# A plan with engine clocks decides the order of issue of routing lists and experts

## Chip, cores and metric

One core of a Trainium2 chip. The metric is the device time of one execution in microseconds (us). TensorE (PE), VectorE (DVE), ScalarE (ACT) and GpSimd (POOL) each run their own instructions in the order in which the program issues them, and wait for one another by semaphores; SyncE (SP) issues most plain transfers.

## What is computed

- Stage A: a two-dimensional Fourier transform of x (8 x 3072 x 256), of which the real part is kept, and the first expert layer, `((x @ w1) * (x @ w2)) @ w3 @ w_out`, for 24576 tokens.
- Stage B, which the change touches: routing and eight experts.

```
logits = x @ w_gate                       # 24576 tokens x 8 experts
for (tok, e) in descending order of logit:
    if tok is free and expert e has fewer than 3072 tokens: assign tok to e
for e in range(8):
    h = max(x[mask_e] @ w1[e], 0);  out[mask_e] = h @ w2[e]
```

The kernel finds the assignment in eight rounds ("lists"): in each one it finds the expert that fills up first and which tokens it takes, then takes that expert and those tokens out.

## The kernel before

**A list** (`route`, line 1122, a generator) has these parts. The set-up (lines 1130 to 1165, VectorE) makes each token's best logit, its expert and a 16-bit key in two halves, and two transposing transfers on SP's queue. Two searches (`search`, line 1094) of eight rounds each look for a threshold; a round is two counts on VectorE (line 1087, 1536 and 864 columns) beside two on ScalarE (line 1084), two small matmuls that add the counts up (lines 1102 and 1103, called "sums" here), and three small VectorE operations that choose the next threshold (lines 1109, 1111, 1114), on which the next counts wait. After the searches, lines 1193 to 1217 choose the expert and mark its tokens, lines 1226 to 1258 number them (with matmuls 1233, 1239, 1242), and lines 1267 to 1283 turn marks into a list of row numbers: three parts, each some 20 VectorE operations, one on ScalarE and 64 small matmuls ("matches", in bursts of 16). Line 1288 writes the finished list `idx`. The eighth list takes whatever is left and has no searches.

**The experts** (loop at line 1590): 8 experts x 6 groups of 512 tokens x 8 steps. A step is `first` (line 1447): six matmuls of 512 columns into `hp`, whose ReLU ScalarE writes as a high half (line 1467) and VectorE as a low half (line 1471); then `second` (line 1478) of the step two before: twelve matmuls of 256 columns. In the second step of each group GpSimd makes the low half instead (line 1462). At steps 4 and 6 `turned` (line 1430) transposes the next group's rows, which ScalarE and VectorE split into halves (lines 1437 and 1441). `chunk` (line 1395) splits a piece of the next expert's weights (ScalarE, then GpSimd), `gather` and `store` fetch and write rows by GpSimd's indirect transfers.

**The head**: the first list has no experts to run beside; TensorE fills it with matmuls that stage A put off (`putoff`, line 1339, matmuls at line 1376), and their operands come back from memory.

**The order** of all instructions is written out by the program itself (`manual_schedule`, line 1556). The list generator yields an estimated VectorE cost after each piece, -2 ahead of matmuls that need VectorE's or ScalarE's result, and -1 after a burst of matches. `lists()` (line 1527), called four times a step, goes on with the list while the estimated clock of VectorE is at most QUEUE ahead of TensorE's, returns after each -1, and at a -2 while the clocks of VectorE or ScalarE are ahead of TensorE's. The two counts of a round are charged 0.95 + 0.45 and 0.6 us on VectorE's clock (lines 1087 to 1088). The halves of `hp` and of the transposed rows are issued a fixed number of calls of `due()` later. At the start of an expert's last group whatever is missing of the next list is issued at once (line 1594).

Of the kernel before, what the change touches and what calls it, by code (L numbers as in the profile page):

```python
# [9 lines left out]
F32 = mybir.dt.float32  # L10
# [12 lines left out]
NT = N // 128  # L23
# [995 lines left out]
def stage_b(ctx, tc, I, out, k):  # L1019
# [16 lines left out]
    CHAIN = 0.45  # L1036
# [27 lines left out]
    clock = {"pe": 0.0, "v": 0.0, "a": 0.0, "d": 0.0}  # L1064

    def use(engine, cost, after=0.0):
        clock[engine] = max(clock[engine], after) + cost
        return clock[engine]


# [3 lines left out]
    def count(T, nx):  # L1074

        acc = cnt[0]
        cnt.reverse()
        ja = rt.tile([128, E * NT], BF, name="ja", bufs=1)  # L1080
        for i, n in enumerate((E * NT, SHARE)):
            a = slice(0, E * NT) if i == 0 else slice(SHARE, E * NT)
            with nc.allow_low_precision(reason="counts of at most 1536 are exact"):
                act.activation(ja[:, a], T[:, a], AF.Sign, bias=nx[:, 2 + i:3 + i], accum_out=acc[:, 2 + 3 * i:3 + 3 * i])  # L1084
            use("a", 1.65 if i == 0 else 0.95)
            jk = junk[i]
            vec.tensor_scalar(jk[:, :n], T[:, :n], nx[:, i:i + 1], None, op0=ALU.is_ge, op1=ALU.add, accum_out=acc[:, i:i + 1])  # L1087
            yield 0.95 + CHAIN if i == 0 else 0.6
        return acc
# [4 lines left out]
    def search(T, thr, name, res, extra):  # L1094

        cur, nx = zero, cc[:, 0]
        for i in range(8):
            acc = yield from count(T, nx)
            yield -2
            then = extra[i]() if i in extra else None  # L1100
            ps = rps(4)
            nc.tensor.matmul(ps, blk, acc[:, 0:4], start=True, stop=False)
            nc.tensor.matmul(ps, half, acc[:, 4:8], start=False, stop=True)
            if then:
                then()
            ps = ps[:, 0:3]
            if i < 7:
                bn = small([5], "bn")
                vec.scalar_tensor_tensor(bn, sg5, cur, cc[:, i + 1], op0=ALU.mult, op1=ALU.add)
            kk, j3 = small([1], "kk"), small([3], "j3")  # L1110
            vec.scalar_tensor_tensor(j3, ps, 1.0, thr, op0=ALU.mult, op1=ALU.is_ge, accum_out=kk)
            if i < 7:
                nx = small([5], "nx")
                vec.scalar_tensor_tensor(nx, sv[:, i], kk, bn, op0=ALU.mult, op1=ALU.add)  # L1114
                cur = nx[:, 4:5]
            else:
                new = small([1], name)
                vec.scalar_tensor_tensor(new, kk, 1.0, cur, op0=ALU.mult, op1=ALU.add)
                cur = new
        res.append(cur)  # L1120

    def route(ph, done):
# [3 lines left out]
        if ph < E - 1:  # L1126

            v = rt.tile([128, NT], F32, name="v", bufs=1)
            v4 = rt.tile([128, 8, NT], BF, name="C8", bufs=1).rearrange("p a j -> p (a j)").bitcast(F32).rearrange("p (a j) -> p a j", a=4)
            vec.tensor_tensor(v4, Lw[:, 0:4], Lw[:, 4:8], op=ALU.max)  # L1130
            vec.tensor_tensor(v4[:, 0:2], v4[:, 0:2], v4[:, 2:4], op=ALU.max)
            vec.tensor_tensor(v, v4[:, 0], v4[:, 1], op=ALU.max)
            yield 1.7
            oh = rt.tile([128, E, NT], BF, name="X8", bufs=1)
            vec.tensor_tensor(oh, Lw, v[:, None, :].to_broadcast(whole(E)), op=ALU.is_equal)
            yield 1.7
            vec.tensor_tensor(oh, oh, rank, op=ALU.mult)
            yield 0.9
            m4 = rt.tile([128, 8, NT], BF, name="C8", bufs=1)[:, :4]
            vec.tensor_tensor(m4, oh[:, 0:4], oh[:, 4:8], op=ALU.max)  # L1140
            vec.tensor_tensor(m4[:, 0:2], m4[:, 0:2], m4[:, 2:4], op=ALU.max)
            code = rt.tile([128, NT], BF, name="code", bufs=1)
            vec.tensor_tensor(code, m4[:, 0], m4[:, 1], op=ALU.max)
            yield 1.0
            vec.tensor_tensor(oh, oh, code[:, None, :].to_broadcast(whole(E)), op=ALU.is_equal)
            yield 0.9

            vi = v.bitcast(I32)
            ky = rt.tile([128, NT], I32, name="ky", bufs=1)
            vec.tensor_scalar(ky, vi, 31, -2147483648, op0=ALU.arith_shift_right, op1=ALU.bitwise_or)  # L1150
            vec.tensor_tensor(ky, ky, vi, op=ALU.bitwise_xor)
            hl = rt.tile([128, 2, NT], U16, name="hlv", bufs=1)
            vec.tensor_tensor(hl, ky.bitcast(U16).rearrange("p (j h) -> p h j", h=2), alive[:, None, :].to_broadcast(whole(2)), op=ALU.mult)
            yield 0.9
# [6 lines left out]
            for i, T in ((1, hT), (0, lT)):  # L1161
# [3 lines left out]
                nc.sync.dma_start(T.rearrange("p (k t) -> p k t", k=12), pl, transpose=True)  # L1165
                yield 0.9
                use("d", 0.0, clock["v"] + 3.4)
            yield -2
# [6 lines left out]
            vec.tensor_scalar(hb, hc, -1.0, -0.5, op0=ALU.mult, op1=ALU.add)  # L1175
            with nc.allow_low_precision(reason="counts of at most 1536 are exact"):
                act.activation(junk[0], hT, AF.Sign, bias=hb, accum_out=acc[:, 2:3])
            vec.scalar_tensor_tensor(lT, hT, hc, lT, op0=ALU.is_equal, op1=ALU.mult)
            yield 1.7
            thr2 = small([3], "thr2")  # L1180

            def rest(acc=acc):
                ps = rps(4)
                nc.tensor.matmul(ps, blk, acc[:, 0:4], start=True, stop=True)
                base = small([1], "base")
                vec.tensor_scalar(base, ps[:, 2:3], 0.5, float(8 * E * NT), op0=ALU.mult, op1=ALU.add)
                vec.scalar_tensor_tensor(thr2, neg3, base, thr1, op0=ALU.mult, op1=ALU.add)

            yield from search(lT, thr2, "lc", res, {0: rest})
# [3 lines left out]
            vec.tensor_scalar(d8[:, 0], id8, hc, None, op0=ALU.mult)  # L1193
            vec.scalar_tensor_tensor(d8[:, 1], id8, lc, id8, op0=ALU.mult, op1=ALU.add)
            yield 0.4
            yield -2
            ps = rps(2 * E)
            nc.tensor.matmul(ps, onesf, d8.rearrange("p a e -> p (a e)"), start=True, stop=True)
            t8 = rt.tile([128, 2, E], F32, name="t8")
            vec.tensor_copy(t8.rearrange("p a e -> p (a e)"), ps)  # L1200
            mh, ml, l8 = small([1], "mh"), small([1], "ml"), small([E], "l8")
            vec.tensor_reduce(mh, t8[:, 0], axis=AX.X, op=ALU.max)
            vec.scalar_tensor_tensor(l8, t8[:, 0], mh, t8[:, 1], op0=ALU.is_equal, op1=ALU.mult)
            vec.tensor_reduce(ml, l8, axis=AX.X, op=ALU.max)
            vec.scalar_tensor_tensor(l8, l8, ml, rank9[:, :E], op0=ALU.is_equal, op1=ALU.mult)
            vec.tensor_reduce(ec, l8, axis=AX.X, op=ALU.max)
            vec.tensor_scalar(ml, ml, 1.0, None, op0=ALU.subtract)
# [24 lines left out]
        for c in range(3):  # L1232
            nc.tensor.matmul(tot[:, c * 128:(c + 1) * 128], m2[:, c * 128:(c + 1) * 128], ones, start=True, stop=True)
# [417 lines left out]
```

## Time and profile before

| what | us |
|---|---|
| time, median of 3 runs | 2791.53 (2791.46 to 2792.09) |
| time of the profiled execution | 2802.85 |
| its span, first to last instruction | 2801.1 |
| stage A ends, the head begins | 1395 |
| first expert's first matmul | 1527 |
| last matmul | 2790 |

Positions are us from the start of the span. The profiled execution is 11.3 us longer than the median of the runs; sums are made against the profiled one and then set back by those 11.3 us. A matmul's end in the trace is modelled, and matmuls overlap: what one costs is the distance between starts.

### The profile page before, as it was taken

To read this page: it belongs to the slowest core of one execution; us is meant where nothing else is said; L and a number is where in the kernel's file an instruction comes from. 1 tells how busy PE (TensorE), PEld (TensorE's weight loads), DVE (VectorE), ACT (ScalarE), POOL (GpSimd) and SP (SyncE) were. 2 spreads that over 40 slices of the span, in tenths; PEclk is the share of its full clock that TensorE was granted. 3 is DMA by queue.
4 is the path that set the end of the run, shared out by engine and by line. 5 is a ranking of instruction groups with operands and counts; after the bars stand their busy time and mean duration, and the time that the engine had idled before them with its cause. 6 is when DMAs were issued, how large, how long until landed. Compare 5 with 4: busy or idle time off the path is not lost.

```text
span 2801.1 us, 51732 instructions
## 1 busy us (share of the span) xinstructions
PE 2666.7 (95%) x19903; PEld 2451.8 (88%) x19903; DVE 2130.4 (76%) x3711; ACT 1317.3 (47%) x2383; POOL 1524.3 (54%) x1529
## 2 busy tenths in 40 slices
PE   4999999999999999999996999989999999999998
PEld 2899999999999999987796888878888888889997
DVE  8788787978878797898877888788787878862222
ACT  2344444444444444444453747555573746543332
POOL 7295775939577593964304345353635436363532
PEclk8999999999999999999997999999999999999999
DMA  6410110111111011145394112211212122121211
GB/s 232 134 54 32 39 47 25 49 37 50 36 39 47 24 47 39 45 159 200 133 330 164 43 61 57 69 50 46 75 45 70 50 67 56 41 69 43 76 46 35
DMA packets 104705, 207.33 MB, mean 74 GB/s; under 512 B 35178, under 2 KB 60442, under 8 KB 99338
## 3 DMA queue, kind: packets, MB, share of 16 engines
q1 hardware_dynamic: 81000, 131.03, 13.7%
q0 software_dynamic: 22224, 72.58, 8.1%
q8 instruction: 157, 2.57, 0.4%
q14 instruction: 90, 0.74, 0.1%
q10 hardware_dynamic: 1234, 0.41, 0.1%
HBM read 118.16 MB, written 80.28 MB: 71 GB/s over the span
## 4 chain that ended last, share of the span: by engine, by line
PE 76%; DVE 15%; issue 3%; ACT 3%; POOL 2%; DMA 1%; another core or an unknown queue 0%; DVEq 0%; POOLq 0%; ACTq 0%; SPq 0%
PE yp L1488 14%; PE l L221 7%; PE l L223 7%; PE l L222 7%; PE hp L221 5%; PE acc L805 5%; PE hp L222 5%; PE hp L223 5%; PE acc L801 4%; PE acc L802 4%; DVE oR L1087 3%; PE l L837 3%; PE hp L1376 1%; ACT ja L1084 1%; DVE qs L860 1%
## 5 line engine op out<-in xcount | busy, mean ns | idle before, releaser
L855 POOL TENSOR_TENSOR al<-qs,ah 128x512 fp32r<-128x512 f32 x376 | 513.2, 1365 | 404.7 <-ACT ah L854 316.4
L1488 PE MATMUL yp<-FA,W 128*128 128x256 f32 x3040 | 621.3, 286 | 15.4 <-DVE W L1471 7.5
L1488 PEld LDWEIGHTS yp<-FA,W 128*128 128x128 f32 x3040 | 496.8, 190 | 37.2 <-DVE W L1471 10.4
L860 DVE TENSOR_TENSOR qs<-pm 128x512 f32<-128x512 f32 x384 | 427.1, 1112 | 41.2 <-DVE pm L844 1.8
L1471 DVE SCALAR_TENSOR_TENSOR W<-hp,W 128x512 fp32r<-128x512 f32 x336 | 230.4, 687 | 233.6 <-ACT W L1467 217.8
L854 ACT ACTIVATE ah<-qs 128x512 fp32r<-128x512 f32 x376 | 237.2, 631 | 354.4 <-DVE qs L860 309.9
L1488 PE MATMUL yp<-FB,W 128*128 128x256 f32 x1520 | 387.4, 282 | 0.0
L843 DVE TENSOR_TENSOR pm<-l,qs 128x512 f32<-128x512 f32 x384 | 264.7, 689 | 150.8 <-PE l L223 117.4
L841 ACT ACTIVATE qs<-l 128x512 f32<-128x512 f32 x384 | 227.3, 592 | 239.2 <-PE l L223 223.9
L221 PE MATMUL hp<-tabA,tabB 128*128 128x512 f32 x768 | 318.1, 414 | 0.9 <-ACT tabA L1437 0.9
L1467 ACT ACTIVATE W<-hp 128x512 fp32r<-128x512 f32 x336 | 199.5, 594 | 253.2 <-PE hp L223 227.3
L1498 POOL DMA_INDIRECT out_dram<-yo,oi x188 | 193.3, 1028 | 223.4 <-DMA out_dram<-yo,oi 210.4
L222 PE MATMUL hp<-tabA,tabB 128*128 128x512 f32 x768 | 303.8, 396 | 8.3 <-DVE tabA L1441 8.3
L1084 ACT ACTIVATE ja<-oR,nx 128x1536 bf16<-128x1536 uint16 x196 | 238.1, 1215 | 139.8 <-DVE nx L1114 125.8
L1488 PEld LDWEIGHTS yp<-FB,W 128*128 128x128 f32 x1520 | 287.4, 189 | 14.3
L801 PE MATMUL acc<-W,ah 128*128 128x264 f32 x1120 | 283.7, 284 | 0.0
L1087 DVE TENSOR_SCALAR_CACHE_REDUCE oR<-oR,nx 128x1536 uint16<-128x1536 uint16 x196 | 280.8, 1460 | 3.5
L802 PE MATMUL acc<-W,ah 128*128 128x264 f32 x1120 | 283.4, 284 | 0.0
L844 DVE TENSOR_TENSOR pm<-l,qs 128x512 f32<-128x512 f32 x384 | 261.1, 680 | 0.0
L1412 POOL DMA_INDIRECT xt<-xs_d,idx x192 | 201.4, 1049 | 109.2 <-issue 50.8
L1462 POOL TENSOR_TENSOR W<-xo,W 128x512 fp32r<-128x512 f32 x48 | 62.1, 1293 | 340.2 <-ACT W L1460 315.1
L223 PE MATMUL hp<-tabA,tabB 128*128 128x512 f32 x624 | 246.0, 394 | 0.0
(346 smaller groups left out, 6894.8 us busy)
## 6 DMA issues: line engine op xcount, KB each, us to landing
xs_d<-xo SPq DMA_DIRECT2D x96, 260.0 KB
xt<-in_xg_dram SPq DMA_DIRECT2D x24, 1024.0 KB
away<-ah SPq DMA_DIRECT2D x56, 256.0 KB
away<-al SPq DMA_DIRECT2D x56, 256.0 KB
yo<-away SPq DMA_DIRECT2D x28, 512.0 KB
raw<-in_w3t_dram SPq DMA_DIRECT2D x16, 512.0 KB
FA<-away SPq DMA_DIRECT2D x14, 512.0 KB
FB<-away SPq DMA_DIRECT2D x14, 512.0 KB
```

Of the source, the lines that this page charges most:

```text
L221: nc.tensor.matmul(out, ah, bh, start=start, stop=False, skip_group_check=True)
L222: nc.tensor.matmul(out, ah, bl, start=False, stop=False, skip_group_check=True)
L223: nc.tensor.matmul(out, al, bh, start=False, stop=stop, skip_group_check=True)
L801: nc.tensor.matmul(acc[i][:, :264], ah[:, a], W[0][:, f], start=f == 0, stop=False, skip_group_check=True)
L802: nc.tensor.matmul(acc[i][:, :264], ah[:, a], W[1][:, f], start=False, stop=False, skip_group_check=True)
L843: vec.tensor_tensor(pm[:, 0].rearrange("p w c -> p (w c)"), ue, qs, op=ALU.add)
L844: vec.tensor_tensor(pm[:, 1].rearrange("p w c -> p (w c)"), ue, qs, op=ALU.subtract)
L855: (vec if n == k.aside - 1 and f in LAST else pool).tensor_tensor(al, qs, ah, op=ALU.subtract)
L860: return ah, al, parts, lambda: vec.tensor_tensor(ab, pm[:, :, 0], pm[:, :, 1], op=ALU.mult)
L1084: act.activation(ja[:, a], T[:, a], AF.Sign, bias=nx[:, 2 + i:3 + i], accum_out=acc[:, 2 + 3 * i:3 + 3 * i])
L1087: vec.tensor_scalar(jk[:, :n], T[:, :n], nx[:, i:i + 1], None, op0=ALU.is_ge, op1=ALU.add, accum_out=acc[:, i:i + 1])
L1488: nc.tensor.matmul(yp[i], hhl[seq[s][0]][:, t[i]], seq[s][1], start=f == 0 and s == 0 and (i % 2 == 0 or len(yp) == 4), stop=f == NF - 1 a ...
```

## The change

Every operation keeps its shape, engine and operands. What is new is who decides when each is issued. Each operation becomes an `Op` with engine, duration, ready time and due time; clocks for TensorE, VectorE and ScalarE move with what is issued, and LAGS says how long after an end another engine can start. GpSimd and the transfers have no clock, but for one entry "d" for the transposing transfers. A list yields sets of operations; a set becomes ready when the set before it has ended. `pick` lets a list operation run on VectorE or ScalarE unless it would make an asked expert operation miss its due time. `burst` issues TensorE's own work, about 0.7 us at a time; only between bursts are list matmuls issued whose planned ready time has come, all of them in a row. The weights of the next expert are fetched as soon as its list names it (from the second group on), and the first group of the next expert as soon as its list is done. In the head the put-off matmuls are issued back to back, 0.476 us at a time. In `store`, ScalarE's copy of the first half becomes ready after half of the last step's matmuls.

```
+    SOON = 0.1
+    LAGS = {"v": 0.1, "a": 0.15, "pe": 0.28, "d": 0.1}
+    clock = {"pe": 0.0, "v": 0.0, "a": 0.0}
...
+    def pick(e):
+        t, l = clock[e], listed(e)
+        known = [o for o in asked[e] if o.ready is not None]
+        x = min(known, key=lambda o: (max(t, o.ready) > t + SOON, o.due)) if known else None
+        if l is None:
+            return None if x is None else (max(t, x.ready), x)
+        at = max(t, l.ready)
+        last = min([o.due - o.dur for o in asked[e]] or [1e9])
+        if x is not None and max(t, x.ready) + x.dur <= at + SOON:
+            return max(t, x.ready), x
+        if at + l.dur <= last or x is None and last > 1e8:
+            return at, l
+        if x is not None:
+            return max(t, x.ready), x
+        return None
...
+    def burst(dur, fn, needs=(), patience=0.05):
+        t = settle(needs)
+        advance(t)
+        while listed("pe") is not None and listed("pe").ready <= t + patience:
+            clock["pe"] = max(clock["pe"], listed("pe").ready)
+            advance_list("pe")
+            t = max(t, clock["pe"])
+            advance(t)
+        clock["pe"] = t
+        fn()
+        clock["pe"] += dur
+        return clock["pe"]
...
-            use("a", 1.65 if i == 0 else 0.95)
-            yield 0.95 + CHAIN if i == 0 else 0.6
+            ops += [("a", 1.58 if i == 0 else 0.84, signs), ("v", n / 960 + 0.14, steps)]
+        yield ops
...
+            yield [("pe", 0.15, sums), ("v", 0.13, base)]
+            yield [("v", 0.35, found)]
...
+            yield [("v", 1.7, largest),
...
+                   ("v", 1.4, ranks),
...
+            yield [("v", 0.8, choice), ("v", 1.7, chosen)]
...
+        yield [("v", 1.3, whereto), ("v", 1.68, lambda: shifts(C8, 1)), ("v", 1.68, lambda: shifts(X8, 0))]
...
+            return [("pe", 0.46, lambda jj0=jj0: some(jj0)) for jj0 in range(0, H, BURST)]
...
+        free["tp"] = [ask(
+            Op("a", 0.5, lambda: act.activation(xh[:, kt], tp, AF.Copy), at + 0.28, at + slack),
+            Op("v", 0.6, lambda: vec.tensor_tensor(xl[:, kt], tp, xh[:, kt], op=ALU.subtract), None, at + slack + 0.4))]
...
+            at = burst(0.7, lambda: mm3(nc, hp, w[0][0][:, kt], w[0][1][:, kt], grp["xh"][:, kt], grp["xl"][:, kt], kt == 0, kt == 1),
+                       [made, grp["turned"][kt]])
...
+            last = ask(Op("a", 0.96, both, at + 0.28, at + 3.0))
...
+            last = ask(Op("a", 0.48, lambda: act.activation(hh, hp, AF.Relu), at + 0.28, at + 1.6),
+                       Op("v", 0.6, lambda: vec.scalar_tensor_tensor(hl, hp, 0.0, hh, op0=ALU.max, op1=ALU.subtract), None, at + 2.6))
...
+        for m in range(0, len(order), 6):
+            at = burst(0.119 * len(order[m:m + 6]), lambda: some(order[m:m + 6]), [hhl[2]] + list(needs))
+            middle(at)
...
-                        while len(done) < ph + 2:
-                            next(gens[0])
-                        st = weights(which[ph + 1])
...
+                    if g and ph + 1 < E and st is None and len(which) > ph + 1:
+                        st, fetched = weights(which[ph + 1]), clock["pe"] + 12.0
...
+                        while f == 3 and len(done) < ph + 2:
+                            idle()
+                        if len(done) > ph + 1:
+                            nxt = group(ph + 1, 0)
...
-                        wnext.append(chunk(st, f))
+                    while g == G - 1 and st is not None and len(wnext) <= f:
+                        wnext.append(chunk(st, len(wnext), fetched, clock["pe"] + 20.0))
```

## Rows read from the trace of the kernel before

**Rows 1.** The page's first part: busy us, share of the span, instructions.
```profile
PE 2666.7 (95%) x19903; PEld 2451.8 (88%) x19903; DVE 2130.4 (76%) x3711; ACT 1317.3 (47%) x2383; POOL 1524.3 (54%) x1529
```

**Rows 2.** Busy time by stretch: head, first, fifth and last expert.
```profile
core 0: us, PE busy (x) PEld busy (x) DVE busy (x) ACT busy (x) POOL busy (x), PEclk, DMA share, GB/s
...
1395.00:1527.20 132.20, 110.55 (x1010) 107.42 (x1011) 98.49 (x242) 61.71 (x103) 21.53 (x33) 0.87 0.75 266
1527.20:1692.70 165.50, 154.24 (x1125) 134.99 (x1124) 141.02 (x302) 95.09 (x162) 73.35 (x75) 0.99 0.20 57
...
2173.00:2333.80 160.80, 154.18 (x1149) 137.38 (x1148) 131.84 (x292) 93.21 (x166) 77.32 (x79) 1.00 0.20 59
...
2646.30:2790.00 143.70, 142.99 (x930) 129.87 (x928) 36.08 (x53) 45.55 (x81) 54.77 (x59) 1.00 0.14 42
```

**Rows 3.** The same for TensorE alone, one group of the last expert.
```profile
2646.30:2669.70 23.40, 23.40 (x155) 1.00 0.21 63
```

**Rows 4.** TensorE's waits from 1527 to 2790: us in total, times, longest.
```profile
PE rps L1102 <- DVE oR L1087: 19.2, 23, 1.5
PE hp L222 <- DVE tabA L1441: 8.3, 7, 4.6
PE yp L1488 <- DVE W L1471: 7.5, 14, 1.7
PE yp L1488 <- POOL W L1462: 5.0, 6, 1.3
PE yp L1488 <- ACT yo L1494: 2.9, 5, 0.7
PE li L1283 <- DVE oC L1275: 1.8, 1, 1.8
```

**Rows 5.** Timeline of matches among an expert's matmuls: start, us, instruction.
```profile
1648.44 0.57 PE L1283 MATMUL li<-oC,oR 128*128 128x48 bf16 x16
1648.86 0.36 PE L1488 MATMUL yp<-FA,W 128*128 128x256 f32 x1
1649.06 0.28 PE L1488 MATMUL yp<-FB,W 128*128 128x256 f32 x1
1649.18 0.28 PE L1488 MATMUL yp<-FA,W 128*128 128x256 f32 x1
```

**Rows 6.** Timeline of one round of a search, in the head.
```profile
1465.81 1.81 DVE L1087 TENSOR_SCALAR_CACHE_REDUCE oR<-oR,nx 128x1536 uint16<-128x1536 uint16 x1
...
1467.54 1.11 DVE L1087 TENSOR_SCALAR_CACHE_REDUCE oR<-oR,nx 128x864 uint16<-128x864 uint16 x1
...
1468.58 0.22 DVE L1109 SCALAR_TENSOR_TENSOR bn<-xt,nx 128x5 f32<-128x5 f32 x1
...
1468.81 0.24 PE L1102 MATMUL rps<-cnt,blk 128*128 128x4 f32 x1
...
1469.20 0.16 DVE L1111 SCALAR_TENSOR_TENSOR j<-rps,thr 128x3 f32<-128x3 f32 x1 [0.40 <-PE rps L1103]
...
1469.73 1.81 DVE L1087 TENSOR_SCALAR_CACHE_REDUCE oR<-oR,nx 128x1536 uint16<-128x1536 uint16 x1
```

**Rows 7.** Timeline: first operations of `choice`, `chosen` and `where`, in the head.
```profile
1482.79 0.17 DVE L1200 COPY t<-rps 128x16 f32<-128x16 f32 x1 [0.55 <-PE rps L1198]
...
1484.19 0.26 DVE L1211 TENSOR_SCALAR one<-code,ec 128x192 bf16<-128x192 bf16 x1
...
1486.36 0.15 DVE L1225 TENSOR_SCALAR wf<-ec 128x1 f32<-128x1 f32 x1
```

**Rows 8.** Timeline: one set-up operation in the head, and beside GpSimd.
```profile
1399.87 0.56 DVE L1140 TENSOR_TENSOR C<-X 128x768 bf16<-128x768 bf16 x1
...
1835.08 1.29 POOL L1462 TENSOR_TENSOR W<-xo,W 128x512 fp32r<-128x512 f32 x1
1835.26 1.53 DVE L1140 TENSOR_TENSOR C<-X 128x768 bf16<-128x768 bf16 x1
```

**Rows 9.** Timeline of the head: TensorE's first put-off matmuls, first sums' result.
```profile
1395.00 8.15 PE L1376 MATMUL hp<-W,tabA 128*128 128x256 f32 x48 [0.30 <-DVE L L895]
1402.99 5.79 PE L1376 MATMUL hp<-W,tabB 128*128 128x256 f32 x48
...
1417.43 0.16 DVE L1111 SCALAR_TENSOR_TENSOR j<-rps,xt 128x3 f32<-128x3 f32 x1 [6.14 <-PE rps L1103]
```

More of the change, by code (lines that the diff above doesn't have):

```diff
@@ new lines, in advance, with force @@
+    def advance(to):
+        while True:
+            best = None
+            for e in ("a", "v"):
+                c = pick(e)
+                if c is not None and c[0] < to and (best is None or c[0] < best[0]):
+                    best = c
+            if best is None:
+                return
+            if listed(best[1].eng) is best[1]:
+                advance_list(best[1].eng)
+            else:
+                emit(best[1])
+    def force(op):
+        while op.end is None:
+            first = next(o for e in asked for o in asked[e] if o is op or (o.then is not None and reaches(o, op)))
+            while first.ready is None:
+                first = next(o for e in asked for o in asked[e] if o.then is first)
+            emit(first)
+        return op.end + LAGS[op.eng]
@@ new lines, in reaches, with settle @@
+    def reaches(o, op):
+        while o is not None and o is not op:
+            o = o.then
+        return o is op
+    def settle(ops):
+        advance(clock["pe"])
+        return max([clock["pe"]] + [force(o) for o in ops])
+    def burst(dur, fn, needs=(), patience=0.05):
[7 more added lines that the diff above has]
+        clock["pe"] = t
+        fn()
+        clock["pe"] += dur
+        return clock["pe"]
@@ L1071, in whole, with idle @@
+    def idle():
+        at = min([listed("pe").ready] if listed("pe") is not None else [clock["pe"] + 0.5])
+        clock["pe"] = max(clock["pe"], at)
+        advance(clock["pe"])
+        while listed("pe") is not None and listed("pe").ready <= clock["pe"]:
+            advance_list("pe")
+            advance(clock["pe"])
     def whole(b):
@@ L1304, in stage_b @@
+            yield [("v", 0.8, taken), ("v", 2.0, closed)]
     xrows = k.xs_d
@@ L1393, in weights, with chunk @@
         return st
-    def chunk(st, f):
-        res = []
+    def chunk(st, f, ready, due):
+        res, made = [], []
         for i in range(2):
@@ L1480, in second @@
+        free["hp"].append(last)
+        return hh, hl, last
+    def second(wts, f, hhl, yp, rows=range(4), needs=(), middle=lambda at: None):
+        wh, wl = (w.rearrange("p k d -> p (k d)") for w in wts[f][0][1])
         seq = [(0, wh), (0, wl), (1, wh)]
@@ new lines, in stage_b, with filler @@
+        more = putoff() if k.putoff else None
+        turn["gen"] = (x for ph in range(E) for x in route(ph, done))
+        proceed()
+        def filler():
+            nonlocal more
+            if next(more, 0) == 0:
+                more = None
+        while not done:
+            if which and st is None:
+                st, fetched = weights(which[0]), clock["pe"] + 12.0
+            if more is not None:
+                burst(0.476, filler, patience=0.25)
+                continue
+            if st is not None and len(wts) < AHEAD and clock["pe"] > fetched:
+                wts.append(chunk(st, len(wts), fetched, 1e6))
+            idle()
```

492 lines of the change are left out of this document (239 added, 253 removed).

## The prediction

> **What bounds the kernel now.** I read the page's first part, then busy time by stretch, then TensorE's waits, then timelines around each kind of wait. TensorE is busy 95% of the span [rows 1], so only its idle time and what interrupts it can be won; VectorE at 76% and ScalarE at 47% matter by when they deliver. The change touches nothing ahead of 1395 us, half of the span. Behind that there are three regimes [rows 2]. The head, 132.2 us, has VectorE's chain as its bound: TensorE has put-off matmuls to do, but the first expert can't start before the list is done. The experts with a list beside them take 165.5 and, in a typical one, 160.8 us. The last one, with no list, takes 143.7 us, and one of its groups 23.40 us with TensorE never idle [rows 3]. Six such groups are 140.4 us; the other 3.3 us of the last expert are its end. So a list costs a typical expert 20.4 us.
>
> How much of that is work? The 192 matches come in 12 bursts of 16, and a burst takes 0.42 us, after which the next two expert matmuls start 0.20 apart where 0.12 is usual [rows 5]: 12 x 0.50 = 6.0 us. The 16 pairs of sums cost some 0.14 us and the same 0.08 of interruption: 3.5 us. The numbering's few matmuls are, by my estimate from these, 1.3 us. That is 10.8 us of work, and 9.6 us of waiting per typical expert, 14.3 us in the first (165.5 - 140.4 - 10.8). Six experts with a searched list: 14.3 + 5 x 9.6 = 62 us. The table of waits gives the second count [rows 4]: six rows hold 44.7 us in 56 waits, counted from the modelled end of the matmul before. A matmul listed with 0.28 us is followed after 0.12 [rows 5], so a wait costs about 0.16 us more than its row: 44.7 + 56 x 0.16 = 54 us. I take 58 us, between the two. The largest row is sums waiting for VectorE's counts, then the transposed rows' low half, then the low half of `hp`, GpSimd's half, the copy of the result, and matches.
>
> **What the plan removes.** The order before charges a round's counts with 0.95 + 0.45 + 0.6 = 2.0 us on VectorE; they take 2.77 us from the first count's start to the operation behind the second [rows 6]. So the sums stand too early in TensorE's order, and VectorE, further behind than its clock says, gets to the experts' halves late. The new plan charges 1.74 + 1.04 = 2.78 us, which is right to 0.01, and it issues a half ahead of a list operation that would make it late. The halves are due 2.6 us (ReLU) or 3.4 to 5.4 us (transposed rows) after their matmuls, while TensorE needs a ReLU two steps later, over 5 us by the 23.40 us of eight steps [rows 3]. The copy of the result now starts half a step earlier, which covers its longest wait of 0.7 us [rows 4]. I therefore let all of the 58 us go except GpSimd's share: GpSimd has no clock in the plan, and its 5.0 us (6.0 with 6 x 0.16) stay. Gain: 52 us; bounds 35 and 58.
>
> Matches: four bursts of a part now follow one another, so a list interrupts the experts at 3 places for them, not 12: 9 x 0.08 = 0.7 us, over the seven lists that run beside experts 5 us.
>
> **The head.** The first sums kept VectorE waiting for 6.14 us [rows 9], where a usual round has 0.40 [rows 6]: 5.7 us lost to put-off matmuls issued ahead of them. The plan puts the sums where the counts end. It doesn't know that TensorE's first 48 matmuls take 8.15 us where the next 48 take 5.79 [rows 9], the granted clock standing at 0.87 over the head [rows 2], so TensorE gets there 2.4 us late: 3.3 us won. The other rounds lose at most a put-off burst of 0.476 us each; bounds 0 and 5 us for all, and I take 2, since the round shown waits only 0.40. The transposing transfers stay ahead of the fetches that they were ahead of on SP's queue; chunk's halves and the four gathers keep their place on GpSimd's. Behind the list the path to the first expert matmul (gather, transposes, halves) is the same. Gain: 5 us.
>
> **What the plan adds: waits for its own errors.** TensorE's order is fixed by planned times, so wherever the real list is later than planned, TensorE waits at the list's next matmul, and the expert's matmuls queue behind it; if TensorE is late, VectorE waits and the two are level again. List matmuls are issued only between bursts of 0.7 us, so a planned result lies on average 0.35 us before its use, and that much lag costs nothing.
>
> - Rounds: the plan has 2.78 + 0.10 + 0.15 + 0.28 + 0.35 = 3.66 us, the trace 3.92 (1465.81 to 1469.73, rows 6). Most of it is the last piece, 0.35 planned and 0.53 real (1469.20 to 1469.73): its operations depend on one another. 0.26 us of lag against a cover between 0 and 0.7 would cost 0.05 us on average; expert halves issued into the same gap take part of that cover. I take 0.15, between 0 and 0.26: 16 rounds x 6 lists x 0.15 = 14 us (0 to 25).
> - Set-up: the plan prices VectorE alone. An operation of 0.56 us in the head took 1.53 us with GpSimd's subtraction beside it [rows 8], 0.97 us more. I take two such hits a list, 2 us, between none and six (5.8 us): 12 us (0 to 35). TensorE pays for them at the first sums.
> - After the searches: `choice` is planned at 0.8 and takes 1.40, `chosen` 1.7 and takes 2.17 us [rows 7]; 1.07 us late, less 0.35 of cover, and half as much again for the numbering and the three parts, which have dependent operations as well: 1.0 to 1.7 us. I take 1.7 a list, between 0 and 3: 10 us (0 to 18).
>
> Together 36 us of new waits. They lie on the path that sets the end, since TensorE has nothing to do in their place. The last list has no searches; I leave it at nothing, covered by TensorE's steps beside it.
>
> **Sum.** 2802.85 - 52 - 5 - 5 + 36 = 2776.9 us for the profiled execution, less 11.3 us for the median: **2765 us**, 0.9% faster. A measurement can tell about 0.2% (5.6 us) from no change.
>
> **Rivals.**
>
> The plan holds (18%). For it: the counts, most of a list's time, are priced to 0.01 us, and the 0.26 us a round mostly fits under a burst. Against it: rows 7 and 8. New waits of 5 us in all, and the same gains: 2802.85 - 62 + 5 - 11.3 = 2735 us; with the upper bounds of the gains (58, 5, 8) 2725.
>
> The lists are the bound anyway (12%). The next expert's rows can be fetched only when its list is done, and the code lets TensorE idle for it in the last group. VectorE is busy 131.84 of 160.80 us in a typical expert [rows 2]; if its work and the waits in the rounds don't fit into less, experts stay at about 160 us, and only the first expert's extra 4.7 us and some of the head come off: 2785 us. Against it: 18% of VectorE is idle, and a round takes 3.92 us when nothing interrupts it.
>
> VectorE falls behind the plan and TensorE waits for all of it (17%, slower). The place is the set-up and the sums of each searched list. If halves fill the gaps so that nothing is covered, a list lags 16 x 0.26 = 4.2 us in the rounds, 3 after them, and with six hits 5.8 in the set-up: 13 us, 78 us over six lists, against 62 removed, so 2807 us. It decides from 62 / 6 = 10.3 us of lag a list. For it: the plan is greedy, so it has no reserve on VectorE; rows 8. Against it: only rows 8 put the set-up that high, and TensorE and VectorE are level again after each sum.
> The Trainium skill, SBUF — State Buffer, section "Who interferes with whom", has a rule that speaks against the change in this way: a VectorE operation with two SBUF inputs and a GpSimd operation that reads SBUF exclude one another, and whichever starts second waits for the whole of the other. The trace agrees: the VectorE operation that started 0.18 us after GpSimd's 1.29 us subtraction was 0.97 us longer. By that rule a plan without a clock for GpSimd can't know these hits, and the set-up, made almost wholly of such operations, would tend to the upper bound and the time to 2807 us.
>
> **How the numbers follow.** The forecast, between 2740 and 2782 by the bounds of its terms taken half way, has 53%; the plan that holds 18%, the lists as the bound 12%, the lagging plan 17%. Faster by over 0.2%: 53 + 18 + 5 of the third = 76%; within 0.2%: the other 7; slower: 17. The range reaches down to 2724, into the second case nearly to its end, and up to 2798, past the third and short of most of the fourth: some 17% is left out.
>
> **What would show it.** Right: sums waiting for counts fall from 19.2 us to under 15; the rows for the transposed half, the `hp` half and the copy fall from 18.7 us together to under 4; GpSimd's half stays near 5; experts with lists take 153 to 157 us and the last ones 140.4; VectorE's wait before the first sums' result in the head falls from 6.14 to about 3 us; first expert matmul near 1522. Waits appear at the first sums of a list and at the numbering. Wrong: experts that still take 160 us with idle time at the last group (the lists), waits of over 10 us a list at the sums (the lag), or new waits for weight halves by GpSimd, since `chunk` may now be issued up to 20 us later.

## The result, and the profile after

The changed kernel takes 2756.51 us (median of 4 runs, 2755.3 to 2759.12). The kernel before, run beside it on the same chip, takes 2791.81 us (2791.46 to 2794.35). The ratio is 0.9874, 95% interval 0.9862 to 0.9886: 35.3 us or 1.3% faster. The forecast was 2765 us with a range from 2724 to 2798.

The profiled execution of after took 2757.3 us, 0.8 more than its median. The one of before took 2802.85 us, and by its time it came from another chip: in a later group of runs a profiled execution of before took 2799.93 beside a median of 2800.81 on its own chip. So the 11.3 us that the prediction set back are a difference between chips, not one between a profiled execution and the others. Below, chip A is that of the result; the experiments ran on three others, B, C and D, on which the kernel before took 2800.81, 2803.02 and 2803.17 us. Times are compared within one chip.

First part of the page, after, and busy time by stretch (columns as in [rows 2]): the head, the first, the fourth and the seventh expert.

```profile
PE 2653.9 (96%) x19903; PEld 2450.7 (89%) x19903; DVE 2104.1 (76%) x3711; ACT 1321.8 (48%) x2383; POOL 1524.5 (55%) x1529
```

```profile
1394.10:1522.35 128.25, 109.95 (x1011) 105.55 (x1011) 101.60 (x250) 58.37 (x91) 18.21 (x26) 0.93 0.79 274
1522.35:1687.50 165.15, 153.64 (x1126) 137.72 (x1124) 135.40 (x298) 98.48 (x175) 79.08 (x83) 0.97 0.20 59
1995.70:2149.40 153.70, 152.85 (x1152) 137.57 (x1151) 132.87 (x306) 98.09 (x171) 79.62 (x81) 1.00 0.21 61
...
2460.60:2601.00 140.40, 140.40 (x915) 127.83 (x913) 37.39 (x55) 50.36 (x94) 68.99 (x79) 1.00 0.19 61
```

The counts of instructions are those of [rows 1]. In the fourth expert TensorE is idle for 0.85 us where a typical one of before had 6.6 [rows 2]. From the starts of the experts' first matmuls:

| | before | after | after, chip D |
|---|---|---|---|
| first expert starts | 1527.2 | 1522.35 | 1522.8 |
| first expert | 165.4 | 165.2 | 164.5 |
| experts 2 to 6, mean | 160.2 | 154.6 | 156.4 |
| expert 7 | 152.5 | 140.4 | 140.4 |
| expert 8 | 143.2 | 143.3 | 143.3 |

The last column belongs to a run of after on chip D, where the kernel before takes 2803.17 us, as long as the profile of before. Its sum is the one to read: head 4.4, first expert 0.9, five experts 5 x 3.8 = 19, expert 7 12.1, together 36.4 us, against 2802.85 - 2766.19 = 36.7 between the profiled executions.

TensorE's waits, after, from 1527 to 2744 us (columns as in [rows 4]):

```profile
PE yp L1647 <- POOL W L1629: 5.9, 1, 5.9
PE rps L1228 <- DVE bn L1235: 3.4, 4, 1.9
PE li L1421 <- DVE oC L1442: 3.4, 3, 1.1
PE yp L1647 <- ACT yo L1656: 1.7, 5, 0.7
PE tp L1606 <- DVE tabA L1612: 1.3, 1, 1.3
PE rps L1228 <- DVE oR L1210: 1.2, 3, 0.5
PE rps L1384 <- DVE wf L1375: 0.8, 3, 0.3
...
PE hp L222 <- DVE tabA L1612: 0.2, 1, 0.2
PE yp L1647 <- DVE W L1634: 0.2, 1, 0.2
```

Read it against [rows 4]. Sums waiting for counts: 19.2 to 1.2, and 3.4 us more in four waits that the profile puts down to `base` (L1235), the small operation that VectorE runs right behind the counts and that ends some 0.15 us after them; the two longest of these, 1.9 and 1.1 us, are at the first sums of a list. The halves and the copy: 18.7 to 2.1. What is new, sums behind `base`, the transposes and the numbering, comes to 6.4 us. GpSimd's row has kept its size, but its six waits have become one, in the first group of the first expert. That wait has a history, in three views: TensorE, GpSimd, ScalarE.

```profile
1532.13 0.28 PE L1647 MATMUL yp<-FB,W 128*128 128x256 f32 x1
1538.27 1.22 PE L1647 MATMUL yp<-FA,W 128*128 128x256 f32 x4 [5.86 <-POOL W L1629]
```

```profile
1523.71 0.74 POOL L1574 TENSOR_TENSOR tabB<-ste,tabB 128x256 fp32r<-128x256 f32 x1 [6.11 <-ACT tabB L1573]
...
1536.97 1.25 POOL L1629 TENSOR_TENSOR W<-xo,W 128x512 fp32r<-128x512 f32 x1
```

```profile
1520.20 0.60 ACT L1611 ACTIVATE tabA<-tp 128x512 fp32r<-128x512 f32 x1 [14.76 <-PE tp L1606]
...
1523.23 0.41 ACT L1573 ACTIVATE tabB<-ste 128x256 fp32r<-128x256 f32 x1
```

From the bottom: ScalarE idles 14.76 us for the first transposes, with weight halves queued behind them; GpSimd idles 6.11 us for these halves, makes the remaining ones and the next gathers first, and starts the half of the second step at 1536.97. The granted clock was 0.50 (the 1.2 GHz level) over the 5.13 us after TensorE's wait, which cost some 2.6 us more. The group takes 31.7 us; in before it took 24.7.

The head, after: the first put-off matmuls, the first sums' result, the end of the list, the last transfer into the table of rows, the first gather.

```profile
1394.11 8.60 PE L1542 MATMUL hp<-W,tabA 128*128 128x256 f32 x48 [0.30 <-DVE L L895]
```

```profile
1413.71 0.16 DVE L1241 SCALAR_TENSOR_TENSOR j<-rps,xt 128x3 f32<-128x3 f32 x1 [3.32 <-PE rps L1229]
...
1505.10 0.28 DVE L1450 SCALAR_TENSOR_TENSOR idx<-ls 128x24 int32<-128x24 f32 x1
```

```profile
1507.44 0.51 SPq L1529 DMA_DIRECT2D xs_d<-md  x1
```

```profile
1510.00 1.60 POOL L1582 DMA_INDIRECT xt<-xs_d,idx  x1 [2.28 <-DVE L L1466]
```

VectorE waits 3.32 us for the first sums, not 6.14 [rows 9], and the list is written at 1505.1, 9.5 us earlier than in before (1514.6). The first gather starts 4.6 us behind the list, though, at 1510.00; in before it was 0.3. It follows the last transfer that completes the table of rows (L1529) by 2.6 us, and by 2.6 or 2.7 in three other profiles of the new order, whenever that transfer came. The gather's row names VectorE's L1466, which ends 0.25 us ahead of the gather; but in the run with late ReLU halves (below) the gather starts at 1509.78, 0.14 us before L1466 ends and 2.56 us behind the transfer, so it is the transfer that it waits for. The last put-off matmul now starts at 1502.9, in before at 1496.3. Of 9.5 us won, 4.9 arrive. The amount differs from one profile to the next: from the first put-off matmul to the first expert's first matmul before took 132.2 and 131.3 us in its two profiles, after 128.2, 125.1 and 126.9 in its three, so the head gained 3 to 7 us.

### The profile page after: what moved, and what is told of

Read it like the earlier page. It is cut to its first block, busy times and chain, and to the rows that moved or that the text cites. A ratio compares the mean times of both kernels' runs of the same rounds, so it can differ in the third digit from the quotient of the medians.

```text
span 2755.5 us, 51811 instructions
## 1 busy us (share of the span) xinstructions
PE 2653.9 (96%) x19903; PEld 2450.7 (89%) x19903; DVE 2104.1 (76%) x3711; ACT 1321.8 (48%) x2383; POOL 1524.5 (55%) x1529
## 3 DMA queue, kind: packets, MB, share of 16 engines
q1 hardware_dynamic: 81000, 131.03, 14.2%
## 5 line engine op out<-in xcount | busy, mean ns | idle before, releaser
L1661 POOL DMA_INDIRECT out_dram<-yo,oi x188 | 214.0, 1139 | 262.5 <-DMA out_dram<-yo,oi 197.0
L221 PE MATMUL l<-eo,SW 128*128 128x256 f32 x768 | 220.7, 287 | 0.0
```

Of the source, the lines that this page charges most:

```text
L221: nc.tensor.matmul(out, ah, bh, start=start, stop=False, skip_group_check=True)
```

## Experiments

Ratios are to the kernel before on the same chip. "Than after" is a difference of medians where after ran beside it, on chips C and D; on chip B it did not, and there the difference of the ratios to 0.9877 (the mean of after's three ratios: 0.9874, 0.988, 0.9876) stands in, times 2800.81 us.

**The prices alone, in the old order.**

```
-            yield 0.95 + CHAIN if i == 0 else 0.6
+            yield 1.74 if i == 0 else 1.04
```

> The kernel before, with one thing changed: the two counts of a round are charged 1.74 and 1.04 us on VectorE's clock in place of 1.40 and 0.60. Theory A (the sums stood too early because the counts were priced too low, and that one price is most of the gain): TensorE's waits for counts fall from 19.2 us to under 8, the waits for the experts' halves fall too, and the time by 15 to 25 us, to 2767 to 2777 us. Theory B (the price alone gives little: what counts is that expert operations have due times and go ahead of list operations): the sums' row falls, the halves' rows stay or grow, as VectorE's work only moves, and the time changes by under 8 us.

2854.93 us (2853.58 to 2856.11), ratio 1.019 (1.0173 to 1.0207): 54 us slower than before, outside what either theory gave. TensorE's waits from 1527 us on, and VectorE's longest in the head (14.2 us in before, 13.3 on this chip):

```profile
PE li L1283 <- DVE oC L1275: 34.8, 14, 2.9
PE yp L1488 <- DVE W L1471: 17.3, 10, 2.9
```

```profile
DVE j L1111 <- PE rps L1103: 33.2, 15, 7.8
```

Sums waiting for counts fell from 19.2 us to 9.7, of which 8.4 are put down to `base`. But `lists()` stops when VectorE's clock is QUEUE ahead, and with true prices it stops more often: the two searches of a list beside experts 2 to 6 take 97 to 99 us together instead of 80 to 82, more of the list is left when the last group begins, and the rest is issued at once there, matches behind the VectorE operations that make their marks (the first row). Experts 1 to 6 take 167 to 171 us, 45 us more than in before on this chip. A further 19 us are lost in the head (first expert's first matmul at 1544.8, 1526.1 in before), because the old program uses the same prices a second time: there it issues put-off matmuls in proportion to them, so the sums stand behind more of them and VectorE waits. Expert 7 is 7.5 us shorter. The low price made up for both rules. So the gain doesn't come from the prices as such; how much each of the two rules costs was seen, not varied.

**The low prices, in the new plan.**

```
-            ops += [("a", 1.58 if i == 0 else 0.84, signs), ("v", n / 960 + 0.14, steps)]
+            ops += [("a", 1.58 if i == 0 else 0.84, signs), ("v", 1.4 if i == 0 else 0.6, steps)]
```

> The changed kernel, with the two counts of a round planned at 1.40 and 0.60 us on VectorE, as before, in place of 1.74 and 1.04. Theory A: each searched list is planned 16 x 0.78 = 12.5 us too short, far over the 0.35 us of cover a round, so the sums' row goes from 4.6 us to 30 to 60 us in total and the time up by as much, to 2785 to 2815 us. Theory B: halves with due times keep most of the gain, sums' row 10 to 20 us, time 2765 to 2775 us.

2815.18 us (2812.41 to 2816.97), ratio 1.0047 (1.003 to 1.0063): some 48 us slower than after. The time is what the first theory gave, its row isn't:

```profile
PE rps L1228 <- DVE bn L1235: 14.3, 29, 2.5
PE li L1421 <- DVE oC L1442: 8.8, 6, 3.6
...
PE rps L1228 <- DVE oR L1210: 5.9, 7, 1.9
PE rps L1384 <- DVE wf L1375: 5.0, 6, 2.3
```

The two rows of sums come to 20.2 us, where after has 4.6 and 30 to 60 were expected. A plan that takes 0.8 us a round off VectorE's clock has TensorE ahead again, as in before. Other waits of lists (numbering and matches) grew too, and the granted clock fell behind some of them, which is counted below.

**Halves due 3 us later.** All of them, and then only the ReLU halves (the last four changed lines).

```
-            Op("a", 0.5, ..., at + 0.28, at + slack),
-            Op("v", 0.6, ..., None, at + slack + 0.4))]
+            Op("a", 0.5, ..., at + 0.28, at + slack + 3.0),
+            Op("v", 0.6, ..., None, at + slack + 3.4))]
...
-            last = ask(Op("a", 0.96, both, at + 0.28, at + 3.0))
-            last = ask(Op("a", 0.48, ..., at + 0.28, at + 1.6), Op("v", 0.6, ..., None, at + 2.6))
+            last = ask(Op("a", 0.96, both, at + 0.28, at + 6.0))
+            last = ask(Op("a", 0.48, ..., at + 0.28, at + 4.6), Op("v", 0.6, ..., None, at + 5.6))
```

> The changed kernel, with the due times of the experts' halves (ReLU, transposed rows, GpSimd's pair) 3 us later, so that list operations go ahead of them more often; prices as they are. Theory A: the ReLU halves were due over 2 us before TensorE needs them, so 3 us eat that reserve: rows for halves 3 to 10 us in place of 0.4, time up by 3 to 10 us. Theory B: the due times are what carries the gain: halves 15 us and more, time up by 15 us and more.

> Of the due times that were made 3 us later before, only the ones of the ReLU halves are later here; the halves of the transposed rows keep theirs. Theory A: TensorE needs a ReLU half two steps after its matmuls, over 5 us, so 3 us more are mostly absorbed: under 15 us slower than the kernel after, and the waits for the halves of the transposed rows (44.6 us when both were late) fall under 5 us. Theory B (the due times matter by the total work that they let the list push aside, whichever half it is): over 35 us slower, with the waits moved to the ReLU halves.

All: 2836.88 us (2833.88 to 2838.91), ratio 1.0124 (1.0107 to 1.0141), some 69 us slower than after. The ReLU halves alone: 2790.19 us (2788.13 to 2792.45), ratio 0.9953 (0.9936 to 0.9969), 22.8 us slower than after beside it. Waits, all halves late:

```profile
PE tp L1606 <- DVE tabA L1612: 22.3, 18, 3.1
PE hp L222 <- DVE tabA L1612: 20.9, 16, 1.9
```

Waits, ReLU halves late (from 1510 us on):

```profile
PE li L1421 <- DVE oC L1442: 10.2, 6, 5.4
PE rps L1228 <- DVE bn L1235: 9.8, 11, 1.9
...
PE hp L222 <- DVE tabA L1612: 3.9, 2, 2.2
...
PE yp L1647 <- DVE W L1634: 3.2, 1, 3.2
```

The transposed rows' waits go with their own due times, from 43.2 us to under 6. The 22.8 us lie between what the two theories gave, and the row of the ReLU halves explains only 3.2 of them. With the halves put off the lists run faster (the two searches take 71 to 78 us together beside experts 2 to 6, where after beside it has 77 to 80) and further ahead of need (the sixth is written 139 us before its expert starts, in after 71), and the waits are for marks and sums instead. So with due times 3 us later more than the whole gain is lost. By the difference of the two runs some two thirds of that hangs on the transposed rows; no run has those alone late.

**After again, on chips C and D,** as the measure for the rest.

> The changed kernel once more, unchanged, on one chip with the three below, so that they are compared with it directly: 0.9874 of the kernel before, within its interval (0.9862 to 0.9886). Its trace also tells whether the 5.9 us wait for GpSimd's half in the first group comes every time (then it is the order of issue) or not.

> The kernel after, unchanged, as the measure for the three kernels beside it. Expected from the two runs so far: ratio to the kernel before 0.986 to 0.989, first group of the first expert 31.7 us. Open is whether the pauses inside rows of 64 matches (9 of them, 4.0 us, on one chip; none in the profile of another) come again. Theory A: they belong to the row's length and come on any chip now and then, so there are some. Theory B: they belong to that chip, so there are none here unless it is the same one.

2768.18 us (2766.68 to 2771.01), ratio 0.988 (0.9863 to 0.9896), and 2767.35 (2765.57 to 2769.6), 0.9876 (0.9859 to 0.9892). The 5.8 and 6.7 us for GpSimd's half come again. Rows of 64 matches paused on both (timeline on chip D):

```profile
1938.58 1.48 PE L1421 MATMUL li<-oC,oR 128*128 128x48 bf16 x52
1940.49 0.28 PE L1421 MATMUL li<-oC,oR 128*128 128x48 bf16 x5 [0.43 <-issue]
1941.22 0.25 PE L1421 MATMUL li<-oC,oR 128*128 128x48 bf16 x3 [0.45 <-issue]
```

**Matches: one burst at a time, and two.** After a burst of matches (after the second) an expert's burst follows.

```
+            match = listed("pe").dur == 0.46
             advance_list("pe")
...
+            if match:
+                break
```

> The changed kernel, but after each burst of 16 matches TensorE goes back to the experts, as before, in place of four bursts in a row. If the prediction's term is right (9 interruptions less a list at 0.08 us, seven lists): 5 us slower than the changed kernel. Rival: matches in a row hold the experts up by 1.7 us at a time and give nothing, or single bursts end the list later: within 2 us, or slower by more than 8.

> At most two bursts of 16 matches in a row, then an expert's burst. Theory A (what one burst at a time cost, some 18 us, came from the list's later end, three expert bursts a part): here only one expert burst of 0.7 us stands inside a part, 3 x 0.7 = 2 us a list, so the lists end about 2 us later, most of the groups keep their start, and the time is within 6 us of the kernel after. Pauses among matches go, since a row has at most 32. Theory B (any break inside a part makes the list miss the step at which the next group is begun): 10 to 20 us slower than the kernel after.

One: 2786.46 us (2781.21 to 2791.8), ratio 0.9938 (0.9918 to 0.9957), 18.3 us slower than after beside it. Two: 2781.59 (2779.78 to 2783.41), 0.9922 (0.9906 to 0.9939), 14.2 slower. The prediction had given this 5 us, for interruptions, and one expert burst inside a part was expected to cost under 6. One part of the cost is the list's end. With two bursts the first list beside an expert is written 1.9 us later (1662.89, after 1660.96). GpSimd's queue in after on this chip, then with two bursts:

```profile
1660.84 0.73 POOL L1574 TENSOR_TENSOR FB<-ste,FA 128x256 fp32r<-128x256 f32 x1
1662.41 1.02 POOL L1582 DMA_INDIRECT xt<-xs_d,idx  x1 [0.84 <-DVE A L1460]
```

```profile
1665.78 1.54 POOL L1632 TENSOR_TENSOR W<-xo,W 128x512 fp32r<-128x512 f32 x1 [3.12 <-ACT W L1631]
1667.47 1.52 POOL L1585 DMA_INDIRECT xt<-xs_d,idx  x1 [0.15 <-POOL W L1632]
```

The list misses the step at which the next group is begun, and its first gather is issued behind a half that waits for ScalarE: 5.1 us later for a list 1.9 us later. TensorE then waits 6.7 us for the rows (0.7 in after), and the last group takes 34.6 us, not 29.8.

That is 4.8 us in expert 1. Experts 2 to 6 lose more, 12.8 us together (159.0 us on average beside 156.4), and TensorE doesn't wait for rows there. Their waits are 5.6 us longer, and behind them the granted clock falls, which it doesn't in after on this chip once the first group is over. One wait for sums, the next 3.3 us, and the 4 us behind those:

```profile
1841.47 0.24 PE L1231 MATMUL rps<-cnt,blk 128*128 128x4 f32 x1 [2.27 <-DVE bn L1238]
```

```profile
1842.30:1845.60 3.30, 3.30 (x11) 0.50 0.11 40
1846.00:1850.00 4.00, 4.00 (x31) 1.00 0.00 0
```

Five such stretches at 0.50, after waits of 2.3 to 3.3 us and after pauses among matches, cost some 10 us in this run. With the waits (33.4 us in experts 1 to 7, 24.8 in after) that is a little more than the 17.2 us between the two profiled executions. The same shows in the other slower kernels: the low clock costs some 26 us in experts 1 to 7 with right prices in the old order, 19 with low prices in the plan, 22 with all halves late and 14 with the ReLU halves late, against 3 in before and 3 to 6 in after (estimates: half of TensorE's busy time at 0.50).

The pauses didn't go with rows of 32 matches (7 of them, 4.5 us); with rows of 16 none shows. In the run with one burst, and in the one with truer prices below, the list's end is so late that a transpose of the next expert's first group reads its buffer 0.7 us before its gather is issued; that part of the computation is changed there.

**Truer prices for the small dependent steps.**

```
-            yield [("v", 0.35, found)]
+            yield [("v", 0.53, found)]
...
-            yield [("v", 0.8, choice), ("v", 1.7, chosen)]
+            yield [("v", 1.4, choice), ("v", 2.17, chosen)]
...
-        yield [("v", 1.3, whereto), ...
+        yield [("v", 1.5, whereto), ...
```

> The changed kernel, with the chains of small dependent VectorE operations planned at what they take: 0.53 us in place of 0.35 for the end of a round, 1.40 in place of 0.80 for choice, 2.17 in place of 1.70 for chosen, 1.50 in place of 1.30 for whereto. If the prediction's new waits are real (0.15 us a round, 1.7 us a list after the searches): sums' and numbering's rows fall from 5.4 us to under 2 and the time by up to 5 us. Rival: cover between bursts takes up the lag, and later planned sums only make lists longer: no change within 3 us.

2781.66 us (2780.44 to 2783.64), ratio 0.9927 (0.991 to 0.9943): 13.5 us slower than after beside it. The rows for sums didn't fall (4.2 and 2.5 us, in after beside it 2.9 and 2.4), the two searches stretched (79 to 85 us together beside experts 2 to 6, in after 77 to 83), and the first list beside an expert missed its step as above (4.9 us of waits for rows, a last group of 34.2 us). Most of the 0.26 us of lag a round that the prediction charged is covered; paying for it in the plan costs more.

**The head: weight halves early, and put-off work first.** In the first, the loop that makes the first expert's weight halves moves ahead of the 10.5 us that the plan allows for the first rows; the second has this and

```
-                burst(0.476, filler, patience=0.25)
+                burst(0.476, filler, patience=-0.2)
```

> The changed kernel; ahead of the first expert the four gathers are issued first and then the halves of the six remaining weight pieces at once, before the planned 10.5 us pass, in place of behind the first transposes. Theory: in the first group GpSimd sat idle for 6.1 us (until 1523.7) because ScalarE's halves stood behind the first transposes in ScalarE's order, and the 5.9 us wait for GpSimd's half of step 1 and the low clock after it come from that. Then the wait goes, the first group takes 25 to 26 us in place of 31.7, and the time falls by 5 to 8 us. Rival: GpSimd has too much to do there in any order (12 subtractions of 0.73 us and eight gathers), the wait stays, or the gathers come later: within 2 us.

> Two edits: the weight halves of the first expert are issued ahead of the wait for its first rows, as tried before, and in the head the list's matmuls are issued only when their planned ready time lies 0.2 us back, not 0.25 us ahead, so that TensorE does put-off work first. Theory A: the first expert's first group falls from 31.7 to about 27 us, the put-off matmuls end 2 to 6 us earlier than in the kernel after beside it and the list in the head 0 to 4 us later; since put-off work is the head's bound now, 4 to 10 us faster than the kernel after. Theory B: the list is as much the head's bound as the put-off work, so what one gains the other loses: within 3 us of the early halves alone, that is 0 to 4 us faster than the kernel after.

Halves early: 2767.51 us (2764.18 to 2770.04), ratio 0.987 (0.9853 to 0.9886), 0.7 less than after beside it, no difference. With put-off work first too: 2768.07 (2765.58 to 2769.15), 0.9875 (0.9858 to 0.9891), 0.7 more, again none. The first step was as expected: the first group fell from 31.7 to 27.0 us, and from 30.9 to 25.3 in the second run, the wait for GpSimd to 2.6 and 1.3 us, the first expert to 160.7 and 159.1. It didn't reach the end. With the early halves alone, the put-off matmuls began 6.0 us later in the profiled execution than in the one of after beside it, though the order ahead of them is the same, the list was 6.1 us and the first expert 7.7 us later; this execution was the longest of its four. In the second run the last put-off matmul started 8.6 us earlier (1494.8), yet the first expert started 2.6 us later (1525.4). GpSimd's, VectorE's and SyncE's timelines tell why:

```profile
1496.71 10.10 POOL L1525 COPY xo<-small 128x8 f32<-128x8 f32 x2 [8.81 <-DMA xs_d<-xo]
...
1513.06 1.75 POOL L1582 DMA_INDIRECT xt<-xs_d,idx  x1 [3.51 <-DVE L L1466]
```

```profile
1502.45 3.31 DVE L1438 TENSOR_SCALAR oR<-X 128x512 bf16<-128x512 bf16 x16
1505.68 0.95 DVE L1442 TENSOR_TENSOR oC<-oC,j 128x1536 bf16<-128x1536 bf16 x1
```

```profile
1510.49 0.51 SPq L1529 DMA_DIRECT2D xs_d<-md  x1
```

Two copies of eight columns, 0.19 us each elsewhere, take 10.1 us: the first one ends at 1506.68, within 0.1 us of the end of a run of VectorE operations without a gap (the marks, L1434 and L1438, and the products, L1442). The last rows, their transfers, and the first gather come that much later. The rest of the gain was lost behind the head: experts 2 to 6 took 157.4 us on average beside 156.4. Neither beats after.

## Why the prediction was right

**What the plan removes: right, over-sized.** By the prediction's method (a row, plus 0.16 us a wait) the rows of [rows 4] other than GpSimd's fell from 39.7 to 6.7 us and from 50 to 13 waits: 33 + 6 = 39 us, where the step took 52, between 35 and 58. One reason is the work of a list, taken at 10.8 us: the fourth expert still takes 13.3 us more than one without a list, with TensorE idle for 0.85, so some 12 us are work. The first count of that step left out expert 7: the eighth list, issued at once in its first group, cost it 12.1 us, a third of the whole gain; now it runs beside expert 6. Expert 7 takes 140.3 or 140.4 us in every run of the new order, with late halves and with low prices too, so this third comes from the lists running on ahead and doesn't hang on either. Both rows that the due times were to remove went as said (8.3 and 7.5 us to 0.2 each, though 4.6 of the 8.3 stood in expert 7 and went with the eighth list). The run with all halves late brings back 20.9 us of the first and 5.0 of the second, so the due times do it. The copy's earlier start, which was to cover its longest wait, didn't: five waits and 0.7 us for the longest, before and after.

**New waits: the term that failed.** 36 us were taken; the new rows hold 6.4 us in 10 waits, 8 us. "0.26 us of lag against a cover between 0 and 0.7": seven waits of sums in 96 rounds, four at `base` and three at the counts, so the cover takes nearly all of it, and the run with truer prices shows that removing the lag doesn't pay. The set-up "tends to the upper bound" by the rule on GpSimd: it didn't, since in this order the set-up mostly misses GpSimd. Where it meets it, the row of [rows 8] repeats itself: three of the five L1285 start 0.3 us behind GpSimd's half of 1.4 us and take 2.74 us, the other two 1.75. The operation of [rows 8] is now L1271, mean 554 ns; in before its mean beside the experts was 1440:

```profile
L1271 DVE TENSOR_TENSOR C<-X 128x768 bf16<-128x768 bf16 x5 | 2.8, 554 | 0.1
```

The numbering leaves 0.8 us of waits, where 10 were taken for the choice and what follows.

The two errors have opposite signs: 13 us too much taken off and 28 too much put on. That the sum's gain, 26 us, lies only 9 us from the 35.3 measured is in part luck. With both errors mended the sum would give 41; of the 6 us that this is too much, 2.6 are the clock behind GpSimd's wait, which the sum has no term for, and the rest isn't told apart.

**GpSimd's 5.0 us stayed, but not as said.** They are one wait of the first group, with a slow clock behind it. The sign to watch was named (weight halves issued later), its place wasn't: the first expert's 14.3 us of waiting were counted as gone, and that expert gained 0.3.

**Matches: right sign, wrong reason.** The 5 us for interruptions can't be seen by themselves. On chip D experts 1 to 7 gain 32 us; TensorE's waits there fall from 45.8 us in 59 to 24.8 in 32, 21 + 4 us by the prediction's method, so some 7 us stand in no wait, and the 5 may be among them. Breaking the rows up costs 14 to 18 us, and of what the profiles show of that, most is waits and the clock behind them, not interruptions.

**The head: right sum, other path.** 5 us were forecast and 4.9 came; 3.32 us at the first sums against "about 3", and the first expert at 1522.35 against "near 1522". That the numbers meet so closely is luck, since the head's length differs by 3 us between profiles of one order. The list won 9.5, and the path behind it wasn't the same, which the prediction had taken it to be: list matmuls ahead of put-off work made the put-off rows late.

**The rivals.** The lists as the bound: experts 2 to 6 take 153.7 to 156.6 us, and the lists end ahead of need, so not in after; edits that end the lists later, however, make the first one or two of them so (matches broken up, truer prices). The lagging plan (2807 us on chip A) is near what the run with low prices becomes: 2815 us on chip B, 2805 by its ratio on chip A. The plan that holds (2735) lies 21 us further on; the first expert's 14.3 us that stayed are the larger part of that.

## What to carry to other kernels

An order written out from engine clocks is worth as much as its prices and its due times: ask for each product when its reader needs it, and let only what is left go to the side work. A price that is wrong in the old order may be what keeps another rule (here a queue limit) harmless, so prices and rules are changed together. Before breaking up a block of side work, look at what its end releases: a list that ended 2 us later cost 5 us at the next fetch. And when waits grow, look at the granted clock behind them: with two bursts it cost as much as the longer waits did.

## What was not expected of the hardware

A run of VectorE's marks and products without a gap shut GpSimd out until it ended: 9.97 us for a copy that takes 0.19 (above), and in after 2.4 us in the same place, where the run ended at 1501.89 and the copy at 1501.94. It isn't only in the head. In after GpSimd's issue of a store, usually 1.0 us, took 3.38 beside sixteen marks and the product behind them:

```profile
1647.05 3.38 POOL L1661 DMA_INDIRECT out_dram<-yo,oi  x1 [1.71 <-DMA out_dram<-yo,oi]
```

```profile
1645.42 3.31 DVE L1438 TENSOR_SCALAR oR<-X 128x512 bf16<-128x512 bf16 x16
1648.65 0.94 DVE L1442 TENSOR_TENSOR oC<-oC,j 128x1536 bf16<-128x1536 bf16 x1
```

The Trainium skill, SBUF — State Buffer, section "Who interferes with whom", says that some VectorE operations, `tensor_scalar` among them, can take the pair of ports that they share with GpSimd, and that the other engine is then blocked for the whole instruction. The traces agree, and go further: GpSimd didn't get in between two instructions of such a run. It isn't so for every run without a gap. In before the same two copies end at 1492.36 and 1494.03, each within 0.1 us of the end of one of two VectorE operations in a row:

```profile
1490.55 1.76 DVE L1258 TENSOR_TENSOR C<-rc,xt 128x1536 bf16<-128x1536 int32 x1
1492.23 1.75 DVE L1258 TENSOR_TENSOR X<-rc,xt 128x1536 bf16<-128x1536 int32 x1
```

```profile
1491.63 2.40 POOL L1359 COPY xo<-small 128x8 f32<-128x8 f32 x2 [2.32 <-DMA xs_d<-xo]
```

What makes the difference is open. The prediction used the rule only for what VectorE loses. No run shows whether the head would gain by a copy on another engine.

Matches in rows of 32 and 64 pause for 0.3 to 1.2 us at a time for nothing that the profile shows: 2.8 to 6.2 us a profile on chips B, C and D, none in the profile of after on chip A, none in rows of 16 among the experts. On chip D no transfer of instructions runs from 1936 to 1943 us, around the pauses shown above. The cause is open. The time of one kernel differs by 0.4% between chips (2791.8 to 2803.2 us), as much as some of the edits.
